# Three edits to the expert loop of a mixture-of-experts kernel: small copies on GpSimd, an early branch hint, another order of products

## The chip, the core and the metric

The kernel runs on one core of a Trainium2 chip. The metric is the time on the device in microseconds, lower is better. A core has five engines that work side by side, each with its own queue of instructions in order: TensorE (PE in the rows; PEld is its weight load), VectorE (DVE), ScalarE (ACT), GpSimd (POOL) and SyncE (SP). They wait for each other through semaphores. A letter q behind an engine's name in a row (PEldq, DVEq) is that engine's sequencer, the part that handles branches, waits and counts.

## The reference

A linear attention, a dense two-layer network and, last, a mixture of experts with 8 experts. The change touches the experts alone:

```
for b, s in tokens:
    fresh_e = argmax(logits[b, s])
    e = fresh_e if s == 0 or local_gate[b, s] < 0.5 else prev_e
    p = softmax(logits[b, s])
    h = relu(x[b, s] @ w1[e])            # 384 -> 1024
    out[b, s] = p[e] * (h @ w2[e])       # 1024 -> 384
```

There are 1536 tokens. The expert that a token goes to depends on the data, so the number of tokens of each expert is known only when the kernel runs.

## The kernel before

The first 300 us or so compute attention, the dense network and the routing; they end with a table of token ids and probabilities for each expert. One expert, which the routing prefers, has 256 of its tokens computed early, and these two results are scattered to the output from `XH` (`e2s`, line 885) at the start of the loop described here.

Then comes a loop over the experts e = 0 to 7, written out in full. Each expert's tokens are worked off in tiles of 128. Tile 0 of every expert is always done; tile t > 0 is guarded by a branch, `tc.If(nts[e] > 2 * t)`, nested in `others(e, t)`, so an expert with few tokens jumps over all of its further tiles. In this data experts 0, 1, 3 and 7 have one tile, 5 and 6 have two, 2 and 4 have three: 14 tiles in all. Where a jump is taken, each engine carries out a short join: it adds to its semaphores what the skipped tiles would have added, so that waits behind the join find the same counts on both ways.

One tile is one call of `step(e, t, before, o)`. It is software pipelined: a step does the first product of its own tile and the second product of the tile before it.

- `first_pe` multiplies the transposed rows x (128 tokens) with w1, 512 columns at a time, into banks 0 and 1. Float32 precision is made from two parts: x and w1 are split into an upper part (`xh`, `w1h`) and a lower part (`xl`, `w1l`), and each half takes nine matmuls, six with `xh` and three with `xl`.
- `first_act` (ScalarE) applies the relu and writes `hs`; in the next step `turn_pe` transposes `hs` (8 transposes into banks 2 and 3), and `turn_split` splits it: ScalarE writes the upper part into `hh`, VectorE the lower part into `hl`.
- `second` multiplies `hh` and `hl` with w2, 24 matmuls into bank 4. The result of bank 4 is fetched one step later again by `result`: ScalarE multiplies it with the tile's probability `cur_p` (line 999), and GpSimd scatters it with the ids (line 1000) to the output by an indirect DMA.
- `xpose_pe` and `xpose_split` transpose gathered rows and split them (ScalarE upper part, VectorE lower part): within the step for a further tile (t > 0), and one expert ahead for the tile 0 of the next expert. `get` issues the gather of rows, an indirect DMA on GpSimd.
- `fill2` splits the weights of the next sets into upper part (ScalarE) and lower part (VectorE, up to 1024 columns each). They are done in the steps of tile 0, six in most of them: one fill of w2 (`fl(0)`), two more of w2 (`fl(1)`), and three of w1 (`fl(2)`) near the end of the step, just ahead of `shift`.
- `shift`, at the very end of a step, moves the ids and probabilities one tile on: `cur_i`, `cur_p` take the values of `nxt_i`, `nxt_p`, and these take the ids and probabilities of the tile just done. Those are four copies of 128x1 on VectorE, and `result` copies `cur_i` into a buffer of its own (`oi`, line 998), also on VectorE.

Within the loop the order of each engine's queue is the order in which the calls are written. Ahead of `second`, a step whose `before` is not None gives TensorE a hint for the next branch: `tc.mark_branch_hint_location` places an instruction that tells TensorE early which way the branch `end{e}.{t + 1}` will go. The step (0, 0) has no `before` and thus no hint. Only TensorE gets hints.

Of the kernel before, what the change touches and what calls it, by code (L numbers as in the profile page):

```python
# [27 lines left out]
KD = DM // 128  # L28
# [3 lines left out]
JMAX = NTOK // 128  # L32
# [68 lines left out]
def moe_kernel(ctx: ExitStack, tc: tile.TileContext, rT, kT, rn, kn, vn, wt, un, gt, w_c, wg, w1, w2,  # L101
               cst, cst_b, out, dbg=None):
    nc = tc.nc
    PE, DVE, ACT, POOL, SP = nc.tensor, nc.vector, nc.scalar, nc.gpsimd, nc.sync
# [8 lines left out]
    B = [BB[:, i] for i in range(8)]  # L113
# [10 lines left out]
    tab = const.tile([128, NE, 2, JMAX + 2], F32, name="tab")  # L124
    tabj = tab[:, :, :, 0:JMAX]
    ids = const.tile([128, NE, JMAX], I32, name="ids")
# [34 lines left out]
    def load_a(e):  # L161
        if e < NE:
            for n in range(2):
                s = slice(n * 512, n * 512 + 512)
                SP.dma_start(out=raws[e % 2][0][:, :, s], in_=r3(w1[e], KD)[:, :, s])

    def load_b(e):
        if e < NE:
            for n in range(2):
                s = slice(n * 4, n * 4 + 4)  # L170
                SP.dma_start(out=raws[e % 2][1][:, s], in_=r3(w2[e], KE)[:, s])
# [20 lines left out]
    def fill2(e, i):  # L192

        a, c = raws[e % 2]
        w1h, w1l, w2h, w2l = sets[(e + 1) % 2]
        if i < 3:
            split(w1h[:, i], w1l[:, i], a[:, i])
        else:
            n = slice((i - 3) * 1024, (i - 2) * 1024)
            split(*(t.rearrange("p k f -> p (k f)")[:, n] for t in (w2h, w2l, c)))  # L200
# [5 lines left out]
    def xpose_pe(x, i):  # L206
        px = r3(B[6 + i][:, 0:DM], KD)
        for k in range(KD):
            PE.transpose(px[:, k, :], x[:, k * 128:(k + 1) * 128], ident)

    def xpose_split(i):
        s = slice(i * 128, i * 128 + 128)
        split(XQ[:, 0, :, s], XQ[:, 1, :, s], r3(B[6 + i][:, 0:DM], KD))

    if True:
# [543 lines left out]
        nts = []  # L759
# [166 lines left out]
        def rows(e, t):  # L926

            return XP[e % 2][:, t % 2] if t else XE[e % 2][:, 0]

        def get(e, t):  # L930
            if e < NE and t < JMAX:
                gather(rows(e, t), ids[:, e, t:t + 1])
# [13 lines left out]
        with tc.manual_schedule():  # L946
            for t in ORDER.split():
                name, *a = t.split(".")
                name, _, e = name.partition(":")
# [6 lines left out]
        (cur_i, nxt_i), (cur_p, nxt_p) = ((t[:, 0:1], t[:, 1:2]) for t in now)  # L956

        def shift(e, t):
            DVE.tensor_copy(out=cur_i, in_=nxt_i)  # L959
            DVE.tensor_copy(out=cur_p, in_=nxt_p)  # L960
            if e is not None:
                DVE.tensor_copy(out=nxt_i, in_=ids[:, e, t:t + 1])
                DVE.tensor_copy(out=nxt_p, in_=tab[:, e, 1, t:t + 1])

        def first_pe(e, i, n):

            w1h, w1l = sets[(e + 1) % 2][:2]
            xh, xl = XT[0]
            t, ns = slice(128 * i, 128 * i + 128), slice(n * 512, n * 512 + 512)
            todo = [(a_, w_, k) for k in range(KD) for a_, w_ in ((xh, w1h), (xh, w1l))] + [(xl, w1h, k) for k in range(KD)]  # L970
            for q, (a_, w_, k) in enumerate(todo):
                PE.matmul(out=B[n], lhsT=a_[:, k, t], rhs=w_[:, k, ns], start=(q == 0), stop=(q == 8))  # L972

        def first_act(n):
            ACT.activation(out=hs[:, n * 512:n * 512 + 512], in_=B[n], func=ACTF.Relu)

        def turn_pe(n):
            pt = r3(B[2 + n], 4)
            for k in range(4):
                f = 4 * n + k  # L980
                PE.transpose(pt[:, k, :], hs[:, f * 128:(f + 1) * 128], ident)

        def turn_split(n):
            f = slice(4 * n, 4 * n + 4)
            split(hh[:, f, 0:128], hl[:, f, 0:128], r3(B[2 + n], 4))

        def second(e):
            w2h, w2l = sets[(e + 1) % 2][2:]
            q = 0
            for n in range(2):  # L990
                for a_, w_ in ((hh, w2h), (hh, w2l), (hl, w2h)):
                    for k in range(4 * n, 4 * n + 4):
                        PE.matmul(out=B[4][:, 0:DM], lhsT=a_[:, k, 0:128], rhs=w_[:, k, :], start=(q == 0), stop=(q == 23))  # L993
                        q += 1

        def result(n):
            o, oi = XO[n]
            DVE.tensor_copy(out=oi, in_=cur_i)  # L998
            ACT.activation(out=o, in_=B[4][:, 0:DM], func=ACTF.Copy, scale=cur_p)  # L999
            POOL.indirect_dma_start(out[:, :], IndirectOffsetOnAxis(ap=oi[:, 0:1], axis=0), o[:, :], None,  # L1000
                                    bounds_check=NTOK - 1, oob_is_err=False)

        def step(e, t, before, o):

            if t:
                xpose_pe(rows(e, t), 1)
            else:
                first_pe(e, 0, 0)
            if before is not None:
                for n in range(2):  # L1010
                    turn_pe(n)
                result(o)
            if t:
                xpose_split(1)
                get(e, t + 1)
                first_pe(e, 1, 0)

            todo = [] if t or e == 0 else [(e, q) for q in range(3, 6)] + [(e + 1, q) for q in range(3) if e + 1 < NE]
            parts = todo[:1], todo[1:3], todo[3:]

            def fl(n):
                for q in parts[n]:
                    fill2(*q)

            fl(0)
            if before is not None:
                for n in range(2):
                    turn_split(n)
            first_act(0)
            first_pe(e, int(t > 0), 1)  # L1030
            fl(1)
            first_act(1)
            if t == 0 and e + 1 < NE:
                xpose_pe(rows(e + 1, 0), 0)
                xpose_split(0)
                get(e + 2, 0)
                get(e + 1, 1)
            if before is not None:

                if t + 1 < JMAX:  # L1040
                    tc.mark_branch_hint_location(f"end{e}.{t + 1}", nts[e] > 2 * t + 2, engines=[PE.engine])
                second(before)
            fl(2)
            if t == 0:
                load_a(e + 3)
                if e:
                    load_b(e + 2)
            shift(e, t)

        def others(e, t):  # L1050
            if t < JMAX:
                with tc.If(nts[e] > 2 * t, label=f"end{e}.{t}"):
                    step(e, t, e, t % 2)
                    others(e, t + 1)
# [5 lines left out]
        for e in range(NE):  # L1060
            step(e, 0, e - 1 if e else None, 2 + e % 2)
            if e + 1 < NE:
                ld_n(e + 1)
            others(e, 1)
        for n in range(2):
            turn_pe(n)
        result(2)
        for n in range(2):
            turn_split(n)
        second(NE - 1)  # L1070
        shift(None, 0)
        result(3)


# [71 lines left out]
```

## Time and profile before

| | us |
|---|---|
| median of 3 runs | 479.41 |
| lowest and highest run | 476.97, 481.84 |
| the profiled execution | 477.66 |
| its span on the core | 475.8 |

Of the span, TensorE's matmuls are busy for 83%, VectorE for 66%, ScalarE and GpSimd for 39% each. The mean granted clock of TensorE is 0.966 of full speed. Times in the rows below count from the start of the span; the expert loop is what lies behind 303 us. Of the time of the profiled execution 1.9 us lie outside its span.

### The profile page before, as it was taken

The numbers are of one execution on the slowest core, as the hardware profiler recorded it, in microseconds if no ns is written. First come the engines' busy times: TensorE is split into PE (matmuls) and PEld (weight loads), VectorE is DVE, ScalarE is ACT, GpSimd is POOL, SyncE is SP. The second block draws the span as 40 slices with busy tenths as digits, with TensorE's granted clock in tenths as the row PEclk, the third lists the DMA queues.
The fourth block names the chain that finished last, engine by engine and source line by source line (L and its number), as shares of the span: only waits on it lengthen the run. The fifth ranks groups of instructions, "written<-read, shape, count | busy, mean of one in ns | idle before, by whom it ended". The sixth has DMA issues, their size and how long they took to land. (4 is left out here: it accounts for less than half of the span.)

```text
span 475.8 us, 8791 instructions
## 1 busy us (share of the span) xinstructions
PE 395.7 (83%) x3297; PEld 359.2 (75%) x3297; DVE 315.1 (66%) x673; ACT 186.9 (39%) x447; POOL 187.6 (39%) x185
## 2 busy tenths in 40 slices
PE   1445497899989989999999889849789979989884
PEld 1444486799789979989999878737678868878774
DVE  7998999946963784787649678717912861546240
ACT  1364255221413522121325244317734752637340
POOL 6769978643622551282303220514322211212210
PEclk9999799999989999999999998959999999999997
DMA  8766165033103305000070392672861484230000
GB/s 257 276 198 210 66 221 178 1 104 120 33 2 112 113 17 171 3 34 3 9 290 3 107 391 100 209 273 65 319 242 44 129 322 152 75 106 17 9 23 15
DMA packets 24849, 59.70 MB, mean 125 GB/s; under 512 B 3994, under 2 KB 10598, under 8 KB 24512
## 3 DMA queue, kind: packets, MB, share of 16 engines
q1 hardware_dynamic: 21856, 50.85, 31.2%
q0 software_dynamic: 2912, 7.88, 4.6%
q8 instruction: 38, 0.62, 0.5%
q14 instruction: 43, 0.35, 0.2%
HBM read 56.35 MB, written 5.70 MB: 130 GB/s over the span
## 5 line engine op out<-in xcount | busy, mean ns | idle before, releaser
L515 PE MATMUL banks<-wh,H 128*128 128x384 f32 x288 | 83.9, 352 | 8.1 <-DVE H L503 6.6
L972 PE MATMUL banks<-w1h,xq 128*128 128x512 f32 x168 | 59.7, 417 | 18.3 <-ACT xq L142 9.0
L515 PEld LDWEIGHTS banks<-wh,H 128*128 128x128 f32 x288 | 53.7, 193 | 10.3 <-DVE H L503 7.5
L147 DVE TENSOR_TENSOR w2l<-wb,w2h 128x1024 fp32r<-128x1024 f32 (+1 forms) x27 | 29.3, 1108 | 45.0 <-ACT w2h L142 45.0
L972 PEld LDWEIGHTS banks<-w1h,xq 128*128 128x128 f32 x168 | 32.4, 193 | 28.5 <-ACT xq L142 9.9
L500 ACT ACTIVATE H<-banks 128x512 fp32r<-128x512 f32 x36 | 21.3, 594 | 79.2 <-PE banks L496 72.5
L515 PE MATMUL banks<-wl,H 128*128 128x384 f32 x144 | 49.3, 342 | 0.0
L993 PE MATMUL banks<-w2h,H 128*128 128x384 f32 x224 | 47.4, 345 | 0.3 <-ACT H L142 0.3
L496 PE MATMUL banks<-xq,wh 128*128 128x256 f32 x216 | 44.8, 306 | 0.4 <-DVE xq L479 0.4
L993 PEld LDWEIGHTS banks<-w2h,H 128*128 128x128 f32 x224 | 40.1, 192 | 1.2 <-ACT H L142 0.5
L496 PEld LDWEIGHTS banks<-xq,wh 128*128 128x128 f32 x216 | 36.9, 207 | 1.1 <-DVE xq L479 0.6
L1000 POOL DMA_INDIRECT out<-xh,oi x9 | 9.7, 1076 | 69.4 <-ACT xh L999 63.0
L503 DVE SCALAR_TENSOR_TENSOR H<-banks,H 128x512 fp32r<-128x512 f32 x36 | 24.5, 685 | 18.5 <-ACT H L500 18.4
L972 PE MATMUL banks<-w1l,xq 128*128 128x512 f32 x84 | 34.2, 407 | 0.3 <-DVE now_i L959 0.2
L147 DVE TENSOR_TENSOR w1l<-wa,w1h 128x512 fp32r<-128x512 f32 (+1 forms) x36 | 32.4, 951 | 0.1
L496 PE MATMUL banks<-xq,wl 128*128 128x256 f32 x108 | 32.2, 298 | 0.0
L496 PE MATMUL banks<-xuh,wh 128*128 128x256 f32 x108 | 31.3, 290 | 0.0
L496 PE MATMUL banks<-xul,wh 128*128 128x256 f32 x108 | 30.6, 284 | 0.5 <-DVE xul L479 0.5
L496 PE MATMUL banks<-xuh,wl 128*128 128x256 f32 x108 | 30.5, 282 | 0.0
L142 ACT ACTIVATE w2h<-wb 128x1024 fp32r<-128x1024 f32 (+1 forms) x33 | 28.5, 903 | 2.5 <-DMA wb<-in_w 2.5
L373 POOL TENSOR_TENSOR cv<-R,c 64x384 f32<-64x384 f32 x19 | 18.8, 992 | 23.7 <-DVE c L368 22.0
L142 ACT ACTIVATE w1h<-wa 128x512 fp32r<-128x512 f32 (+1 forms) x36 | 28.1, 856 | 0.0
(234 smaller groups left out, 948.5 us busy)
## 6 DMA issues: line engine op xcount, KB each, us to landing
wa<-in_w SPq DMA_DIRECT2D x16, 768.0 KB, 8.1
wb<-in_w SPq DMA_DIRECT2D x16, 768.0 KB, 10.6
wq<-in_w_c SPq DMA_DIRECT2D x12, 768.0 KB, 6.0
r<-in_rT SPq DMA_DIRECT2D x12, 256.0 KB, 3.3
k<-in_kT SPq DMA_DIRECT2D x12, 256.0 KB, 5.5
rn<-in_rn SPq DMA_DIRECT2D x12, 192.0 KB, 3.9
R<-in_vn SPq DMA_DIRECT2D x24, 96.0 KB, 2.5
kn<-in_kn SPq DMA_DIRECT2D x12, 192.0 KB, 3.1
```

The source lines that it names most:

```text
L142: ACT.activation(out=dst_hi, in_=src, func=ACTF.Relu if relu else ACTF.Copy)
L147: (lo_eng or DVE).tensor_tensor(out=dst_lo, in0=src, in1=dst_hi.bitcast(F32), op=ALU.subtract)
L373: e.tensor_tensor(out=r3(cv[b][s], NH), in0=r3(R[b][g % 2][s, q, :], NH), in1=bc(c[s], [64, NH, HD]), op=ALU.mult)
L496: PE.matmul(out=ph[:, i, :], lhsT=a, rhs=x_[:, k, :], start=(q == 0), stop=(q == 8))
L500: ACT.activation(out=hh[:, ring(n)], in_=r3(B[3 + n % 2], 2), func=ACTF.Relu)
L503: DVE.scalar_tensor_tensor(out=hl[:, ring(n)], in0=r3(B[3 + n % 2], 2), scalar=0.0, in1=hh[:, ring(n)].bitcast(F32), op0=ALU.max, op1=ALU. ...
L515: PE.matmul(out=bank_o(b, g), lhsT=a[:, f2, s][:, i], rhs=w_[:, 2 * p + i, DM:], start=(p + i + n == 0), stop=(p == NP - 1 and i == 1 and ...
L972: PE.matmul(out=B[n], lhsT=a_[:, k, t], rhs=w_[:, k, ns], start=(q == 0), stop=(q == 8))
L993: PE.matmul(out=B[4][:, 0:DM], lhsT=a_[:, k, 0:128], rhs=w_[:, k, :], start=(q == 0), stop=(q == 23))
L1000: POOL.indirect_dma_start(out[:, :], IndirectOffsetOnAxis(ap=oi[:, 0:1], axis=0), o[:, :], None, bounds_check=NTOK - 1, oob_is_err=False)
```

## The change

The four copies of `shift` and the copy of `result` go from VectorE's queue to GpSimd's. The hint is a function of its own, `hint(e, t)`; in the step (0, 0) it now stands ahead of the first products, and elsewhere where it stood. `first_pe` takes several halves: for a further tile (t > 0) it does the six products with `xh` of both halves, then the three with `xl` of both. For a tile 0 the order stays as it was.

```diff
         def shift(e, t):
-            DVE.tensor_copy(out=cur_i, in_=nxt_i)
-            DVE.tensor_copy(out=cur_p, in_=nxt_p)
+            POOL.tensor_copy(out=cur_i, in_=nxt_i)
+            POOL.tensor_copy(out=cur_p, in_=nxt_p)
             if e is not None:
-                DVE.tensor_copy(out=nxt_i, in_=ids[:, e, t:t + 1])
-                DVE.tensor_copy(out=nxt_p, in_=tab[:, e, 1, t:t + 1])
-
-        def first_pe(e, i, n):
+                POOL.tensor_copy(out=nxt_i, in_=ids[:, e, t:t + 1])
+                POOL.tensor_copy(out=nxt_p, in_=tab[:, e, 1, t:t + 1])
+
+        def first_pe(e, i, *halves):
...
-            todo = [(a_, w_, k) for k in range(KD) for a_, w_ in ((xh, w1h), (xh, w1l))] + [(xl, w1h, k) for k in range(KD)]
-            for q, (a_, w_, k) in enumerate(todo):
-                PE.matmul(out=B[n], lhsT=a_[:, k, t], rhs=w_[:, k, ns], start=(q == 0), stop=(q == 8))
+            t = slice(128 * i, 128 * i + 128)
+            for last in range(2):
+                todo = [(xl, w1h, k) for k in range(KD)] if last else [(xh, w_, k) for k in range(KD) for w_ in (w1h, w1l)]
+                for n in halves:
+                    for q, (a_, w_, k) in enumerate(todo):
+                        PE.matmul(out=B[n], lhsT=a_[:, k, t], rhs=w_[:, k, n * 512:n * 512 + 512],
+                                  start=(last == 0 and q == 0), stop=(last == 1 and q == KD - 1))
...
         def result(n):
             o, oi = XO[n]
-            DVE.tensor_copy(out=oi, in_=cur_i)
+            POOL.tensor_copy(out=oi, in_=cur_i)
...
+        def hint(e, t):
+
+            if t + 1 < JMAX:
+                tc.mark_branch_hint_location(f"end{e}.{t + 1}", nts[e] > 2 * t + 2, engines=[PE.engine])
+
         def step(e, t, before, o):
...
             else:
+                if before is None:
+                    hint(e, t)
                 first_pe(e, 0, 0)
...
-                first_pe(e, 1, 0)
+                first_pe(e, 1, 0, 1)
...
-            first_pe(e, int(t > 0), 1)
+            if t == 0:
+                first_pe(e, 0, 1)
...
             if before is not None:
-
-                if t + 1 < JMAX:
-                    tc.mark_branch_hint_location(f"end{e}.{t + 1}", nts[e] > 2 * t + 2, engines=[PE.engine])
+                hint(e, t)
                 second(before)
```

## Rows read from the trace of the kernel before

**Rows 1.** Waits of TensorE from 300 us on: total us, times, longest.

```profile
PE banks L972 <- ACT xq L142: 9.0, 4, 2.6
PE banks L972 <- PEq L1052: 8.0, 5, 6.3
PE banks L209 <- DMA x<-xd,ids: 3.7, 3, 1.6
```

**Rows 2.** Timeline, expert 2 into its tile 1: start, us, engine, line, operation [idle before].

```profile
337.75 2.04 ACT L142 ACTIVATE w1h<-wa 128x1024 fp32r<-128x1024 f32 x2
337.97 3.48 DVE L147 TENSOR_TENSOR w1l<-wa,w1h 128x1024 fp32r<-128x1024 f32 x3
...
339.04 1.04 PE L981 MATMUL banks<-cs,hs 128*128 128x128 f32 x8
...
341.44 0.14 DVE L960 COPY now_p<-now_p 128x1 f32<-128x1 f32 x1
...
341.66 0.58 ACT L999 ACTIVATE x<-banks,now_p 128x384 f32<-128x384 f32 x1 [1.88 <-issue]
...
342.65 0.56 DVE L147 TENSOR_TENSOR xq<-banks,xq 128x384 fp32r<-128x384 f32 x1 [0.23 <-ACT xq L142]
...
342.67 0.50 PE L972 MATMUL banks<-w1h,xq 128*128 128x512 f32 x1 [2.59 <-ACT xq L142]
...
343.23 1.03 POOL L1000 DMA_INDIRECT out<-x,oi  x1 [7.04 <-DVE xq L147]
...
344.18 0.87 PE L972 MATMUL banks<-w1h,xq 128*128 128x512 f32 x3
```

**Rows 3.** Timeline, expert 5 into its tile 1.

```profile
414.06 2.98 ACT L142 ACTIVATE w1h<-wa 128x1024 fp32r<-128x1024 f32 x3
...
416.96 1.04 PE L981 MATMUL banks<-cs,hs 128*128 128x128 f32 x8
...
418.88 0.58 ACT L999 ACTIVATE x<-banks,now_p 128x384 f32<-128x384 f32 x1 [1.84 <-PE banks L981]
...
419.89 0.50 PE L972 MATMUL banks<-w1h,xq 128*128 128x512 f32 x1 [1.90 <-ACT xq L142]
```

**Rows 4.** Timeline, the steps (1, 0) and (2, 0), after the jumps of experts 0 and 1.

```profile
319.27 0.58 ACT L999 ACTIVATE xh<-banks,now_p 128x384 f32<-128x384 f32 x1 [8.74 <-DMA out<-xh,top_i]
...
331.17 0.86 PEld L981 LDWEIGHTS banks<-cs,hs 128*128 128x128 f32 x8 [0.34 <-DVEq L1052]
...
331.20 0.58 ACT L999 ACTIVATE xh<-banks,now_p 128x384 f32<-128x384 f32 x1 [2.83 <-DVEq L1052]
```

**Rows 5.** The guard's line, 308 to 317 us: ns min/median/max, first and last start.

```profile
L1052 POOLq EVENT_SEMAPHORE  x3: 17/43/5851, 313.7 to 313.9; - x3
L1052 PEldq COMPARE_BRANCH  x1: 6236/6236/6236, 309.9 to 309.9; - x1
```

**Rows 6.** The guard's line, 455 to 463 us, the jump of expert 7.

```profile
L1052 ACTq COMPARE_BRANCH  x1: 50/50/50, 456.4 to 456.4; - x1
...
L1052 DVEq COMPARE_BRANCH  x1: 62/62/62, 459.0 to 459.0; - x1
...
L1052 DVEq EVENT_SEMAPHORE  x1: 21/21/21, 462.0 to 462.0; - x1
```

**Rows 7.** Timeline, the jump of expert 7 and behind it.

```profile
457.24 0.61 ACT L975 ACTIVATE hs<-banks 128x512 f32<-128x512 f32 x1
...
462.14 1.06 PE L981 MATMUL banks<-cs,hs 128*128 128x128 f32 x8 [1.65 <-DVEq L1052]
```

**Rows 8.** Stretch of the last products: us, busy of PE, PEld, DVE, ACT, POOL, PEclk, DMA.

```profile
464.00:468.00 4.00, 4.00 (x16) 4.00 (x15) 1.03 (x5) 0.00 (x0) 0.13 (x1) 0.57 0.02 5
```

**Rows 9.** Small GpSimd operations of line 461: ns min/median/max.

```profile
L461 POOL TENSOR_SCALAR rs<-sq x12: 190/191/596, 35.3 to 231.3; 128x1 f32<-128x1 f32 x12
```

**Rows 10.** Timeline, an operation of line 462 and VectorE beside it.

```profile
77.86 0.96 DVE L299 TENSOR_TENSOR wl<-d,wh 128x768 fp32r<-128x768 f32 x1
...
78.08 1.15 POOL L462 TENSOR_TENSOR rs<-rs,mhalf 128x1 f32<-128x1 f32 x1
```

More of the change, by code (lines that the diff above doesn't have):

```diff
@@ L958, in shift @@
         def shift(e, t):
-            DVE.tensor_copy(out=cur_i, in_=nxt_i)
-            DVE.tensor_copy(out=cur_p, in_=nxt_p)
+            POOL.tensor_copy(out=cur_i, in_=nxt_i)
+            POOL.tensor_copy(out=cur_p, in_=nxt_p)
             if e is not None:
-                DVE.tensor_copy(out=nxt_i, in_=ids[:, e, t:t + 1])
-                DVE.tensor_copy(out=nxt_p, in_=tab[:, e, 1, t:t + 1])
-        def first_pe(e, i, n):
+                POOL.tensor_copy(out=nxt_i, in_=ids[:, e, t:t + 1])
+                POOL.tensor_copy(out=nxt_p, in_=tab[:, e, 1, t:t + 1])
+        def first_pe(e, i, *halves):
             w1h, w1l = sets[(e + 1) % 2][:2]
             xh, xl = XT[0]
-            t, ns = slice(128 * i, 128 * i + 128), slice(n * 512, n * 512 + 512)
-            todo = [(a_, w_, k) for k in range(KD) for a_, w_ in ((xh, w1h), (xh, w1l))] + [(xl, w1h, k) for k in range(KD)]
-            for q, (a_, w_, k) in enumerate(todo):
-                PE.matmul(out=B[n], lhsT=a_[:, k, t], rhs=w_[:, k, ns], start=(q == 0), stop=(q == 8))
+            t = slice(128 * i, 128 * i + 128)
[5 more added lines that the diff above has]
+                                  start=(last == 0 and q == 0), stop=(last == 1 and q == KD - 1))
         def first_act(n):
```

## The prediction

> **What bounds the kernel now.** The table shows TensorE as the busiest engine, and the change touches nothing ahead of the expert loop, so I read the loop alone. First the waits of TensorE there [rows 1]. Three causes are nearly all of them: 9.0 us in four waits for ScalarE's upper part of x, 8.0 us behind the guard's branch, 6.3 of them at one place, and 3.7 us in three waits for gathered rows. All else TensorE does back to back, so a microsecond counts where it shortens one of these. Next, the timeline at each of them, to see what is late there.
>
> The four waits for x are the four entries into a tile 1 (experts 2, 4, 5 and 6). Expert 2 shows the chain [rows 2]. TensorE has finished its transposes at 339.04 + 1.04 = 340.08 and stands until 342.67. It waits for ScalarE's split of x, which is queued behind the multiplication by `cur_p` (line 999). That one starts at 341.66, just 0.08 us after `shift`'s second copy ends (341.44 + 0.14). And the copy stands in VectorE's queue behind three fills of w1l that run until 337.97 + 3.48 = 341.45. So a copy of 128 numbers holds up the product until VectorE has done its fills. ScalarE itself was free at 337.75 + 2.04 = 339.79. Expert 4 repeats the pattern of expert 2, expert 6 that of expert 5 [rows 3].
>
> **Part 1: the copies on GpSimd.** Removed from VectorE: five copies a step of about 0.15 us. Added on GpSimd: the same five, for which the nearest small operation takes 0.19 us, at worst 0.60 [rows 9]. GpSimd has its gathers and scatters and little else here; in a tile 0 its copies stand behind two gathers, in a further tile behind a scatter and a gather, each about 1 us, and the values are wanted one step (some 10 us) later. At these prices they are hidden. If that cover were gone, each microsecond that `cur_p` came after ScalarE is free would be one on the path, up to today's wait.
>
> *Entries of experts 2 and 4.* Without the wait the multiplication starts when ScalarE is free, at 339.79, and the product follows 342.67 - 341.66 = 1.01 us later as now: 340.80 for 342.67, 1.87 gained. There is more: after the jump of expert 1 ScalarE now idles 2.83 us, until 331.20, because line 999 waits for VectorE's join, which comes after its copies [rows 4]. With `cur_p` on GpSimd this goes, and ScalarE's queue, thus its fills, moves up by what TensorE's transposes allow, by my count about 0.9 us. Then TensorE's own transposes end last, and the whole 2.59 us [rows 2] go. Bounds 1.87 and 2.59; I take 2.5, since 0.9 is more than the 0.72 that are missing: 5.0 for the two.
>
> *Entries of experts 5 and 6.* Here ScalarE is free at 414.06 + 2.98 = 417.04, the product could start at 418.05, the transposes end at 416.96 + 1.04 = 418.00: 418.05 for 419.89 [rows 3]. That is 1.84, and 3.7 for two.
>
> *Third tiles (experts 2 and 4).* TensorE waits for gathered rows; of the 3.7 us [rows 1] the longest, 1.6, is in expert 0, ahead of the loop's first branch, which leaves 2.1. The gather is queued behind the scatter, and the scatter starts only at 343.23, when VectorE's split of x has ended (342.65 + 0.56), though its data were there at 342.24 [rows 2]: its wait on VectorE, for `oi`, is counted with a later instruction. With `oi` on GpSimd it goes right after line 999: about 0.7 us earlier against TensorE. But gathers share the DMA engines with the loads of weights. Bounds 0 and 2.1; I take 1.2, nearer to 0.7 for each.
>
> *Jumps of experts 1 and 3.* TensorE's transposes wait 0.34 us for VectorE's join behind the copies [rows 4]. 0.2 each, bounds 0 and 0.34: 0.4.
>
> *The last jump.* VectorE branches at 459.0, behind its copies, and joins at 462.0 [rows 6]; it has no hint. TensorE waits 1.65 us for that [rows 7]. Where nothing holds its sequencer, an engine branches ahead of its last work: ScalarE at 456.4, its last activation starts at 457.24 [rows 6, 7]. So without the copies VectorE branches once its last fill is handed over, by my estimate 1.5 us earlier, and TensorE's own last product is then as late as the join. Bounds 0.4 (the copies' own time) and 1.65; I take 1.5. Behind it, from 464 to 468, the granted clock is 0.57 [rows 8]: TensorE is at 1.2 GHz for most of it, after the 1.65 us of idling, 1.06 us of transposes and another short wait. Four microseconds at 0.57 lose 4.0 x 0.43 = 1.7. With the gap gone I expect the clock to stay up, but a gap of 1.9 to 2.6 us elsewhere lowered nothing, so I can't be sure of the link. Bounds 0 and 1.7; I take 1.5. Together 3.0.
>
> **Part 2: the hint in the step (0, 0).** The branch of expert 0 takes TensorE 6236 ns [rows 5], the largest single stall in the loop. With the hint some 6.5 us ahead of it the stall should go. I still count nearly nothing. In the next step ScalarE stands 8.74 us at line 999, until 319.27, because the buffer that it writes is being read by the scatter of the early results, whose DMA has not landed [rows 4]. Behind it in ScalarE's queue are the split of `hs`, without which `second` can't start, and all fills of this step. TensorE would do its two halves early and then wait there instead, with the clock down. What is left is ScalarE's own short wait for the transposes behind line 999, 0.4 us. Against that: line 999 now waits for GpSimd's join, and GpSimd's join there sits in a wait of 5851 ns from 313.9, until 319.75 [rows 5]. If the copies' count is added behind that wait, line 999 is 0.5 to 1.1 us late. Bounds -1.1 and +0.5; I take -0.1. Where the stall goes: to line 999, behind a scatter that the change doesn't touch.
>
> **Part 3: `xh` ahead in further tiles.** The same 18 matmuls. Today `xl` is there in time: VectorE ends it at 343.21, and TensorE, which starts at 342.67, comes to it six matmuls later, at 344.18 [rows 2]. After part 1 TensorE starts at 340.1 and VectorE's split of x still stands behind its fills: it ends between 341.1 and 342.0. The old order would come to it at 341.6, the new one six matmuls, 1.5 us, later. So this part has no price today and is what covers part 1; without it up to 0.4 us would go back at each of experts 2 and 4. The first half of `hs` comes 1.5 us later for it, and the next reader is a whole `second` away. 0.
>
> **Sum.** 5.0 + 3.7 + 1.2 + 0.4 + 3.0 - 0.1 = 13.2. The profiled execution takes 477.66; it lies 1.75 under the median of the runs. 477.66 - 13.2 = 464.5 for it, 479.41 - 13.2 = 466.2 for the median. With all lower bounds: 3.7 + 3.6 + 0 + 0 + 0.4 - 1.1 = 6.6; with all upper ones 5.2 + 3.8 + 2.1 + 0.7 + 3.35 + 0.5 = 15.7.
>
> **The rivals.**
>
> *GpSimd is locked out (474.5).* Small GpSimd operations take 0.19 us as a rule [rows 9]. One of line 462 took 1.15: it starts 0.22 us into a VectorE operation that reads two tiles in SBUF, and ends 0.41 us after it [rows 10]. The fills of w1l and w2l are such operations, back to back. If the copies get in only when VectorE pauses, `cur_p` comes when it does now, and all of the entries' 8.7 goes: 13.2 - 8.7 = 4.5, thus 474.9, or with a few collisions more 474.5 to 476. What speaks against it: in experts 5 and 6 the copies fall ahead of the fills, and one slot between two fills is enough. The Trainium skill has this as a rule (SBUF — State Buffer, section "Who interferes with whom"): a VectorE instruction with two SBUF inputs contends with a GpSimd instruction that reads SBUF, and the one that issues later blocks for the whole of the other. By that rule a waiting copy goes in at the end of a fill; the rows above agree with the blocking, and no row shows who goes first when both wait. Chance 0.12.
>
> *The hint pays in full (460).* If line 999 of the step (1, 0) did not have to wait for the scatter, the 6.3 us would go, down to 460. The wait's releaser in the trace speaks against it [rows 4]; a shift in the order of GpSimd's first DMAs would speak for it. Chance 0.07.
>
> *GpSimd's join on the path (slower, 482).* Line 999, the first work of ScalarE behind each of the 8 jumps, now needs GpSimd's join, and this queue waits at the join for its DMAs [rows 5]. Today nothing waits for it. Were it 2 us behind TensorE's join at all 8 jumps, 16 us would come on top of the gain: 479.41 - 13.2 + 16 = 482. It decides from the point where the gathers land later than TensorE ends `second`; with a wait as long as 5.85 us this is near at the jumps out of a tile 0, and far at those out of further tiles. Chance 0.06.
>
> *It doesn't do what it says (479).* The hint does not take and ScalarE waits for some other count of VectorE at the entries. The 0.08 us between copy and line 999 speak against it. Chance 0.05.
>
> **How the numbers follow.** Forecast 466.2, chance 0.70; its own range is 463 to 472.8, from the bounds of the sum. The range that I give adds the 2 us by which the runs differ and takes in most of the lock-out: 460.5 to 474.5. One per cent, 4.8 us, is about what a measurement of this kernel can tell from no change: faster is under 474.6. The forecast and the full hint are faster (0.77), and so is a part of the lock-out (0.05): 0.82. The rest of the lock-out and no effect: 0.12. Slower: the join, 0.06.
>
> **What would show it.** Right: line 999 of the entries starts as ScalarE's last fill ends, and TensorE's wait for x shrinks from 9.0 us to under 1; VectorE's last join comes before 461; the first branch is short, but line 999 of the step (1, 0) still starts near 319. Wrong: a small copy on GpSimd of a microsecond or more, line 999 released by GpSimd, or TensorE at 1.2 GHz in another place than before.

## The result and the profile after

| | before | after |
|---|---|---|
| median, us | 479.59 (4 runs) | 466.12 (4 runs) |
| lowest and highest run | 476.97, 481.84 | 465.41, 466.47 |
| the profiled execution, its span | 477.66, 475.8 | 466.47, 464.7 |
| mean granted clock | 0.966 | 0.961 |

The ratio is 0.9719, with a 95% interval of 0.9668 to 0.977: faster by 13.5 us by the medians, with a forecast of 13.2 and 466.2. In the changed kernel `shift` is at lines 959 to 963, the first products at 974, the relu at 978, the transposes of `hs` at 984, the second product at 996, `result` at 1001 (ids), 1002 (ScalarE) and 1003 (scatter), the guard at 1061.

To compare executions I count from the first product of the step (0, 0), "the loop's start" below. From there to the end of the span it is 475.8 - 303.37 = 172.43 us before and 464.7 - 305.46 = 159.24 after: 13.19 gained, to within the 0.1 us to which a span is given. A median counts every run; a ratio leaves out the few runs in a slower state of the chip (one of `early_mix`'s six).

The waits of TensorE from 300 us on in the kernel after, to be held against [rows 1] (total us, times, longest):

```profile
PE banks L974 <- ACTq L1061: 3.4, 3, 2.1
PE banks L209 <- DMA x<-xd,ids: 2.2, 2, 1.8
PE banks L974 <- PEq L1061: 1.9, 4, 0.5
PE banks L996 <- ACT H L142: 1.7, 2, 1.4
```

The wait of 9.0 us for ScalarE's part of x is gone, and of the 8.0 us behind the guard 1.9 are left. The wait for ScalarE's sequencer behind the guard has grown from 0.7 to 3.4 us, and that for ScalarE's split of `hs` ahead of the second product from 0.3 to 1.7. First the entry of expert 2 into its tile 1, in the timeline of the kernel after (start, us, engine, line, operation), against [rows 2]:

```profile
338.32 2.99 ACT L142 ACTIVATE w1h<-wa 128x1024 fp32r<-128x1024 f32 x3
...
339.09 0.17 POOL L960 COPY now_p<-now_p 128x1 f32<-128x1 f32 x1
...
339.48 3.49 DVE L147 TENSOR_TENSOR w1l<-wa,w1h 128x1024 fp32r<-128x1024 f32 x3
...
341.18 0.60 ACT L1002 ACTIVATE x<-banks,now_p 128x384 f32<-128x384 f32 x1
341.26 1.04 PE L984 MATMUL banks<-cs,hs 128*128 128x128 f32 x8
...
342.21 0.50 PE L974 MATMUL banks<-w1h,xq 128*128 128x512 f32 x1
...
342.88 0.55 DVE L147 TENSOR_TENSOR xq<-banks,xq 128x384 fp32r<-128x384 f32 x1
...
343.23 1.03 POOL L1003 DMA_INDIRECT out<-x,oi  x1 [2.49 <-ACT H L142]
...
344.57 1.03 POOL L203 DMA_INDIRECT x<-xd,ids  x1 [0.31 <-issue]
```

The probability is in place at 339.26, two microseconds before ScalarE wants it; line 1002 starts as ScalarE's last fill ends, and TensorE goes from its transposes, which end at 342.30, to the first product at 342.21 without a wait (ends are modelled). The gather for the next tile starts at 344.57, 2.36 behind that product. VectorE still has its fills in front of its split of x, and nothing of this step waits for them.

The two jumps at the loop's start look otherwise (timeline after, the steps (1, 0) and (2, 0)), against [rows 4]:

```profile
313.23 0.80 PE L974 MATMUL banks<-w1h,xq 128*128 128x512 f32 x1 [0.90 <-ACTq L1061]
...
321.07 0.58 ACT L1002 ACTIVATE xh<-banks,now_p 128x384 f32<-128x384 f32 x1 [8.21 <-DMA out<-xh,top_i]
...
323.13 0.96 PE L996 MATMUL banks<-w2h,H 128*128 128x384 f32 x4 [1.39 <-ACT H L142]
...
326.67 2.98 ACT L142 ACTIVATE w1h<-wa 128x1024 fp32r<-128x1024 f32 x3
...
327.80 3.55 DVE L147 TENSOR_TENSOR w1l<-wa,w1h 128x1024 fp32r<-128x1024 f32 x3
...
329.07 1.18 POOL L960 COPY now_p<-now_p 128x1 f32<-128x1 f32 x1
...
329.75 0.79 PE L974 MATMUL banks<-w1h,xq 128*128 128x512 f32 x1 [2.13 <-ACTq L1061]
...
331.58 0.58 ACT L1002 ACTIVATE xh<-banks,now_p 128x384 f32<-128x384 f32 x1 [1.93 <-POOLq L1061]
...
334.13 1.09 ACT L142 ACTIVATE H<-banks 128x512 fp32r<-128x512 f32 x2 [1.02 <-issue]
```

and the guard's line at the jumps of expert 0 (first row) and expert 7 (ns min/median/max, first and last start), against [rows 5, 6]:

```profile
L1061 PEldq COMPARE_BRANCH  x1: 469/469/469, 312.2 to 312.2; - x1
...
L1061 DVEq COMPARE_BRANCH  x1: 63/63/63, 448.6 to 448.6; - x1
L1061 DVEq EVENT_SEMAPHORE  x1: 21/21/21, 450.0 to 450.0; - x1
```

The hint takes: 469 ns for 6236. But line 1002 of the step (1, 0) still stands, for 8.21 us, until the early results have landed, and the second product waits behind it. At the jump of expert 1 TensorE stands 2.13 us and starts 0.10 us after ScalarE's last fill of w1h (326.67 + 2.98 = 329.65); before it was 0.10 us too (325.39 + 2.98 = 328.37, and 328.47). There the copy of the probability took 1.18 us beside VectorE's fills, and line 1002 was released by GpSimd's join. At the last jump VectorE needs 1.4 us from branch to join, 3.0 before.

Last the clock (stretches of the kernel after: us, busy of PE, PEld, DVE, ACT, POOL, PEclk, DMA), against [rows 8]:

```profile
313.00:318.00 5.00, 4.77 (x13) 3.80 (x14) 0.45 (x1) 0.00 (x0) 2.54 (x6) 0.50 1.03 394
...
329.50:334.00 4.50, 4.25 (x15) 3.44 (x16) 2.65 (x3) 1.68 (x3) 2.63 (x5) 0.62 0.36 107
...
335.00:458.00 123.00, 119.46 (x646) 105.48 (x644) 58.85 (x69) 67.07 (x105) 42.48 (x91) 1.00 0.38 138
...
454.00:458.00 4.00, 3.82 (x22) 3.50 (x21) 0.64 (x2) 0.09 (x1) 0.70 (x4) 1.00 0.02 5
```

TensorE ends at full clock now, and instead has a stretch at 0.62, thus mostly 1.2 GHz, behind its 2.13 us at the jump of expert 1. From 335 us to its end it is at full clock throughout.

### The profile page after: what moved, and what is told of

Same layout as the page of the kernel before. It is cut to its first block, busy times and chain, and to the rows that moved or that the text cites. A ratio compares the mean times of both kernels' runs of the same rounds, so it can differ in the third digit from the quotient of the medians.

```text
span 464.7 us, 8778 instructions
## 1 busy us (share of the span) xinstructions
PE 397.1 (85%) x3297; PEld 361.0 (78%) x3297; DVE 310.7 (67%) x600; ACT 186.7 (40%) x447; POOL 205.6 (44%) x258
## 5 line engine op out<-in xcount | busy, mean ns | idle before, releaser
L515 PE MATMUL banks<-wh,H 128*128 128x384 f32 x288 | 86.2, 361 | 8.7 <-DVE H L503 6.5
L974 PE MATMUL banks<-w1h,xq 128*128 128x512 f32 x168 | 61.0, 425 | 5.8 <-ACTq L1061 3.4
L515 PEld LDWEIGHTS banks<-wh,H 128*128 128x128 f32 x288 | 55.6, 199 | 11.0 <-DVE H L503 7.5
L515 PE MATMUL banks<-wl,H 128*128 128x384 f32 x144 | 50.4, 350 | 0.0
L996 PE MATMUL banks<-w2h,H 128*128 128x384 f32 x224 | 46.4, 339 | 1.7 <-ACT H L142 1.7
L496 PE MATMUL banks<-xq,wh 128*128 128x256 f32 x216 | 41.8, 292 | 0.4 <-DVE xq L479 0.4
L996 PEld LDWEIGHTS banks<-w2h,H 128*128 128x128 f32 x224 | 39.1, 188 | 2.9 <-ACT H L142 2.2
L496 PEld LDWEIGHTS banks<-xq,wh 128*128 128x128 f32 x216 | 34.4, 193 | 1.1 <-DVE xq L479 0.6
L974 PE MATMUL banks<-w1l,xq 128*128 128x512 f32 x84 | 34.8, 414 | 0.2 <-DVEq L1061 0.2
L496 PE MATMUL banks<-xq,wl 128*128 128x256 f32 x108 | 30.7, 284 | 0.0
L515 PEld LDWEIGHTS banks<-wl,H 128*128 128x128 f32 x144 | 28.8, 200 | 0.0
```

The lines of the kernel that those rows point to most:

```text
L496: PE.matmul(out=ph[:, i, :], lhsT=a, rhs=x_[:, k, :], start=(q == 0), stop=(q == 8))
L515: PE.matmul(out=bank_o(b, g), lhsT=a[:, f2, s][:, i], rhs=w_[:, 2 * p + i, DM:], start=(p + i + n == 0), stop=(p == NP - 1 and i == 1 and ...
L974: PE.matmul(out=B[n], lhsT=a_[:, k, t], rhs=w_[:, k, n * 512:n * 512 + 512], start=(last == 0 and q == 0), stop=(last == 1 and q == KD - 1))
```

## The experiments

Four questions: is it GpSimd that brings the gain, or the place in the queue; what the other two parts are worth; what the hint is lost to; and what happens to the copies beside VectorE's fills. Times are medians, ratios are to the kernel before on the same chip, and "loop" counts from the loop's start in the profiled execution (before 172.4, after 159.2).

**Each part alone.** `copies_alone` is the kernel before with the copies on GpSimd:

```diff
-            DVE.tensor_copy(out=cur_i, in_=nxt_i)
+            POOL.tensor_copy(out=cur_i, in_=nxt_i)
...
-            DVE.tensor_copy(out=oi, in_=cur_i)
+            POOL.tensor_copy(out=oi, in_=cur_i)
```

> The five small copies on GpSimd, no hint in the step (0, 0), the old order of products. Theory (the copies are the gain): ratio 0.97 to 0.975, 12 to 14 us less than before; the expert loop, from its first product to the end of the span, about 159 us against 172.4 before and 159.2 with all three edits. TensorE's waits for the upper part of x shrink from 9.0 us to under 1. Rival (the hint carries a good part): 3 us or more slower than all three edits together.

467.11 us, ratio 0.9714 (0.967 to 0.9757), loop 159.11. The whole gain is in this part. With the old order TensorE goes from the first product of expert 2's tile 1 to the second product in 4.32 us, as before and after: no wait for the lower part of x.

`hint_alone` is the kernel before with the hint in the step (0, 0):

```diff
             else:
+                if before is None:
+                    tc.mark_branch_hint_location(f"end{e}.{t + 1}", nts[e] > 2 * t + 2, engines=[PE.engine])
                 first_pe(e, 0, 0)
```

> The hint in the step (0, 0) alone. Theory (line 999 of the step (1, 0) waits for the scatter of the early results anyway): the branch goes from 6.2 us to under 0.6, the first product of the step (1, 0) starts some 5 us earlier, and the whole gains 0 to 1 us; ratio 0.998 to 1.002. Rival (the hint pays in full): 6 us less, ratio 0.987.

479.80 us, ratio 0.9988 (0.9959 to 1.0016), loop 172.9. The waits of ScalarE and of TensorE in it:

```profile
ACT xh L999 <- DMA out<-xh,top_i: 9.2, 1, 9.2
```

```profile
PE banks L993 <- ACT H L142: 2.8, 2, 2.4
```

The transposes of the step (1, 0) come 5.2 us earlier (11.72 us behind the loop's start for 16.88), the second product 1.75 (18.60 for 20.35), the first product of expert 2 not at all (25.21 for 25.10).

`no_hint` is the kernel after without this call of `hint`:

```diff
             else:
-                if before is None:
-                    hint(e, t)
                 first_pe(e, 0, 0)
```

> All three edits but the hint in the step (0, 0). Theory: as with all three, loop within 1 us of 159.2. The hint made TensorE idle twice at other places, with the clock down from 313 to 318 and again from 329.5 to 334; without it one low stretch behind the 6.2 us of the branch is left, so it may even be up to 1 us less. Rival (the hint pays once the copies are off VectorE): 3 us or more above all three edits.

466.43 us, ratio 0.971 (0.9674 to 0.9746), loop 159.04: no difference from the whole change.

`order_alone` is the kernel before with the products in the new order:

```diff
...
-                first_pe(e, 1, 0)
+                first_pe(e, 1, 0, 1)
...
-            first_pe(e, int(t > 0), 1)
+            if t == 0:
+                first_pe(e, 0, 1)
```

> The upper part of x ahead in further tiles, alone. Theory: VectorE's lower part is in time with either order, so no change: ratio 0.998 to 1.002, loop within 0.3 us of 172.4. Rival (the order saves a wait today): 0.5 us less at each of six further tiles, 3 us.

479.05 us, ratio 0.9981 (0.9951 to 1.001), loop 172.34: nothing.

**The engine or the place.** `early_shift` is the kernel before, with `shift` still on VectorE and called right behind `result`, ahead of the fills:

```diff
                 result(o)
+                shift(e, t)
...
-            shift(e, t)
+            if before is None:
+                shift(e, t)
```

> The kernel before with one edit: `shift` stays on VectorE and is called right behind `result`, ahead of the fills, not at the end of the step. Theory (what cost the time is the place in VectorE's queue, behind three fills): the four entries and the last jump gain as with the copies on GpSimd; only the gain at the third tiles, which comes from `oi`, is missing. Loop 159.5 to 161.5, ratio 0.973 to 0.978. Rival (VectorE's load or its share of the port is the cost): loop above 165.

465.02 us, ratio 0.9733 (0.9699 to 0.9767), loop 161.8, 0.3 above the range expected. At the entry of expert 2 TensorE's transposes of `hs` now start 0.94 us ahead of the first product, for 0.95 in the kernel after and 3.63 before. So for the entries the copies need not leave VectorE; they have to leave the place behind its fills. One small wait is new, in the list of TensorE's weight loads:

```profile
PEld banks L972 <- DVE xq L147: 2.1, 4, 0.5
```

Here the copy of `cur_p` waits for line 999 and VectorE's split of x stands behind it, so the old order of products comes too early for `xl`: 4.67 us from first to second product for 4.32, at four entries.

`oi_on_dve` is the kernel after with the ids for the scatter copied on VectorE:

```diff
-            POOL.tensor_copy(out=oi, in_=cur_i)
+            DVE.tensor_copy(out=oi, in_=cur_i)
```

> All three edits, but the copy of `result` (`oi`) back on VectorE. Theory (the scatter of a tile 1 waits for a later instruction of VectorE, and the gather of the third tile is queued behind it): in experts 2 and 4 the gather is issued 0.5 to 0.8 us later, TensorE's waits for gathered rows grow by 0.5 to 1.5 us, loop 159.7 to 160.7. Rival (the gather's landing is set by the loads of weights): loop within 0.3 us of 159.2.

466.97 us, ratio 0.9784 (0.9745 to 0.9823), loop 162.6, 1.9 above the range expected. At expert 2's entry (timeline):

```profile
336.44 3.48 DVE L147 TENSOR_TENSOR w1l<-wa,w1h 128x1024 fp32r<-128x1024 f32 x3
...
337.65 1.18 POOL L960 COPY now_p<-now_p 128x1 f32<-128x1 f32 x1
338.77 1.19 POOL L962 COPY now_i<-ids 128x1 int32<-128x1 int32 x1
338.86 0.58 ACT L1002 ACTIVATE x<-banks,now_p 128x384 f32<-128x384 f32 x1 [0.62 <-POOL now_p L960]
```

The lock-out of the first rival, here at an entry: the copies met three fills back to back, and each came through only once a fill had ended. ScalarE stood 0.62 us of TensorE's 2.43 there for it, and the clock fell behind that gap (5.75 us from first to second product). The gather for the third tile starts 2.61 and 2.93 us behind its tile's first product (experts 2 and 4), for 2.36 and 1.94 in the kernel after.

**What the hint is lost to.** My theory: line 1002 of the step (1, 0) writes `XH[1]`, which the scatter of the early results is still reading. The rival: it waits for GpSimd's join, where the untaken tiles' scatters are made up for. `own_buffer` gives this result another of the four buffers:

```diff
-            step(e, 0, e - 1 if e else None, 2 + e % 2)
+            step(e, 0, e - 1 if e else None, 1 if e == 1 else 2 + e % 2)
```

> All three edits, and the result of the step (1, 0) goes into another buffer, which no early scatter reads. Theory (the scatter of the early results is what makes the hint worthless): line 1002 of the step (1, 0) starts when GpSimd has joined, 13.3 us after the loop's first product and not 15.6; the loop is 1.5 to 2.5 us shorter than 159.2. Rival (the weight fills behind it set the pace anyway): loop within 0.5 us of 159.2.

465.57 us, ratio 0.9729 (0.9687 to 0.9772), loop 160.9, longer than either expectation, and the line still waits (timeline, and the guard's line):

```profile
320.13 0.58 ACT L1002 ACTIVATE x<-banks,now_p 128x384 f32<-128x384 f32 x1 [9.57 <-DMA out<-xh,top_i]
...
L1061 POOLq INC_SWDGE_SEM  x1: 408/408/408, 319.6 to 319.6; - x1
```

The timeline names the landing again, but the times do not fit it. The scatter issued at 313.24 lands 6.0 us later, at 319.2, and the line starts 0.9 us after that, 0.15 us behind the last count that GpSimd adds in its join (319.57 + 0.41 = 319.98). In the kernel after the scatter issued at 315.15 lands at 320.96, the line starts at 321.07, and that count of the join begins only at 321.51.

`early_all` is `early_shift` with the hint and this buffer, so that no copy on GpSimd is left:

```diff
+                if before is None:
+                    tc.mark_branch_hint_location(f"end{e}.{t + 1}", nts[e] > 2 * t + 2, engines=[PE.engine])
...
-            step(e, 0, e - 1 if e else None, 2 + e % 2)
+            step(e, 0, e - 1 if e else None, 1 if e == 1 else 2 + e % 2)
```

> `shift` on VectorE ahead of the fills, the hint in the step (0, 0), and the buffer of its own for the result of the step (1, 0). Theory: line 999 of the step (1, 0) then waits for VectorE's join alone, about 8.5 us after the loop's first product and not 15.6, and the 6.2 us of the branch are worth something: loop 154 to 157.5, ratio 0.962 to 0.970. Rival (TensorE's low clock or the fills take it back): loop as with the early shift alone, 160 to 161.

467.26 us, ratio 0.9783 (0.9742 to 0.9823), loop 162.2, again above both; the line waits 9.33 us, by the timeline for the same landing, by the times again until 0.15 us behind that count. By these two the buffer seemed to be out. But the buffer taken, `XR[1]`, is also written and scattered in the untaken tiles, and their count is made up for in the join: one wait was exchanged for the next. `fresh_buffer` is the kernel after with a fifth tile that nothing else uses:

```diff
-            XO.extend(zip((*XR, *XH), (cl.tile([128, 1], I32, name=f"oi{n}") for n in range(4))))
+            xo4 = cl.tile([128, DM], F32, name="xo4")
+            XO.extend(zip((*XR, *XH, xo4), (cl.tile([128, 1], I32, name=f"oi{n}") for n in range(5))))
...
-            step(e, 0, e - 1 if e else None, 2 + e % 2)
+            step(e, 0, e - 1 if e else None, 4 if e == 1 else 2 + e % 2)
```

> All of the change, but the result of expert 1's first tile goes into a buffer of its own, which no earlier scatter reads and which no skipped tile uses. What ScalarE's copy of that result waits for at its 8.2 us wait in the changed kernel is disputed. If it waits for a buffer that the scatter ahead is still reading, it now starts some 13.3 us behind the loop's first product, as GpSimd's copies are done, instead of 15.6, and the loop gets shorter by up to 2 us: 157 to 157.5 us instead of 159.2. If it waits for GpSimd's own join behind the untaken tiles, where the count of the scatters not run is made up, nothing changes: copy at 15 to 16 us, loop 159.0 to 159.5, total 465 to 467.

466.42 us, ratio 0.9722 (0.9677 to 0.9767), loop 159.3.

```profile
ACT xo L1003 <- POOLq L1062: 4.5, 1, 4.5
```

Now the line goes at GpSimd's join, 13.4 us behind the loop's start for 15.6. It was the buffer after all; the next wait in line is GpSimd's. `early_mix` has `shift` early on VectorE and all else as the kernel after:

```diff
-            POOL.tensor_copy(out=cur_i, in_=nxt_i)
+            DVE.tensor_copy(out=cur_i, in_=nxt_i)
...
                 result(o)
+                shift(e, t)
...
```

> The four copies stay on VectorE but are called right behind the result of the tile before, ahead of the fills; the copy of the ids for the scatter on GpSimd, the hint and the new order of the products as in the change. If the place in the queue was the cost and not the engine, the four entries give what the change gave (TensorE waits under 0.1 us for the lower part of x, 4.31 us from the first product of the new tile to the second product instead of the 4.65 of the early copies with the old order), and no copy can be held up by GpSimd's port: loop 158 to 159.5 us, total 464 to 466. If GpSimd is what the gain needs, the entries lose 0.3 to 2 us each again: loop over 161.

467.24 us, ratio 0.9727 (0.9669 to 0.9786), loop 158.75; 4.32 us from first to second product at the entries of experts 2 and 4, so the wait for `xl` is gone. Two edits can have done that, the new order and the copy of the ids on GpSimd: VectorE's split of x ends 1.51 us behind the first product, for 1.70 in `early_shift`, and the old order comes to it after 1.51. `early_fresh` is `early_mix` with the fifth tile:

```diff
...
-            step(e, 0, e - 1 if e else None, 2 + e % 2)
+            step(e, 0, e - 1 if e else None, 4 if e == 1 else 2 + e % 2)
```

> As the kernel with early copies on VectorE and the rest of the change, and in addition the result of expert 1's first tile has a buffer of its own. If the wait at the first jump is for the buffer and for GpSimd's copies together, ScalarE's copy of the result goes at VectorE's own join, 8.1 to 8.5 us behind the loop's first product, and the loop is 154 to 157 us, total 459 to 463. If it is for the landing of the scatter, or for GpSimd's join, by way of the copied ids or of the scatter's count, it stays at 13 to 16 us and the loop at 158 to 159.5.

464.32 us, ratio 0.968 (0.9639 to 0.9721), loop 158.7: the line moves, the loop stays. Timeline of the step (1, 0):

```profile
314.92 0.58 ACT L1003 ACTIVATE xo<-banks,now_p 128x384 f32<-128x384 f32 x1 [2.59 <-DVEq L1064]
...
322.02 0.18 POOL L1002 COPY oi<-now_i 128x1 int32<-128x1 int32 x1 [5.14 <-DMA out<-xh,top_i]
322.24 0.15 DVE L960 COPY now_i<-now_i 128x1 int32<-128x1 int32 x1 [9.00 <-POOL oi L1002]
...
324.47 1.01 PE L997 MATMUL banks<-w2h,H 128*128 128x384 f32 x2 [3.14 <-DVE H L147]
```

The line goes at VectorE's join, 9.5 us behind the loop's start. But VectorE may not overwrite `cur_i` before GpSimd has copied it, GpSimd stands behind the landing, and the lower part of `hs` stands behind VectorE. `early_split` takes this away too: `oi` on VectorE in every tile 0.

```diff
-        def result(n):
+        def result(n, V=POOL):
...
-            POOL.tensor_copy(out=oi, in_=cur_i)
+            V.tensor_copy(out=oi, in_=cur_i)
...
-                result(o)
+                result(o, POOL if t else DVE)
```

> As the kernel with early copies on VectorE and a buffer of its own for expert 1's first result, and the copy of the ids for the scatter is on VectorE as well in every expert's first tile, and on GpSimd in the further ones. In that kernel VectorE stood 9.0 us behind GpSimd's copy of the ids, which waited for a scatter to land, and gave back there the 3.4 us by which the second product had started earlier. If that copy is what is late next, VectorE now goes on at its own join, some 9.5 us behind the loop's first product, the second product of expert 0's third tile runs through without a wait, the first product of expert 2 starts 19.5 to 22 us behind the loop's first product instead of 24.7, and the loop is 153.5 to 156.5 us: total 459 to 463. If the landing of the scatter comes out again at the next jump (GpSimd's gathers for expert 2's further tiles, or a buffer that is still being scattered), the start of expert 2's second tile stays at 35 to 36 us and the loop at 158 to 159.5, total 464 to 466.

466.96 us, ratio 0.9759 (0.9716 to 0.9802), loop 159.4.

```profile
335.30 1.03 POOL L1004 DMA_INDIRECT out<-xh,oi  x1 [6.21 <-ACT w1h L142]
...
341.85 1.04 POOL L1004 DMA_INDIRECT out<-x,oi  x1 [1.76 <-DMA out<-xh,oi]
343.19 1.02 POOL L203 DMA_INDIRECT x<-xd,ids  x1 [0.30 <-issue]
...
349.54 0.55 PE L209 MATMUL banks<-cs,x 128*128 128x128 f32 x3 [2.64 <-DMA x<-xd,ids]
```

Where the time went is seen in the positions (us behind the loop's start, from the timelines):

| | line of `result` (1, 0) | second product (1, 0) | first product (2, 0) | first product (2, 1) | transposes of `hs` (2, 2) |
|---|---|---|---|---|---|
| before | 15.9 | 20.4 | 25.1 | 39.3 | 49.7 |
| after | 15.6 | 17.7 | 24.3 | 36.8 | 45.9 |
| `fresh_buffer` | 13.4 | 17.0 | 22.1 | 34.8 | 45.1 |
| `early_fresh` | 9.5 | 14.3 | 24.7 | 35.8 | 44.6 |
| `early_split` | 10.1 | 16.8 | 21.4 | 32.8 | 44.6 |

`early_split` is 4.0 us ahead of the kernel after at expert 2's tile 1, and 1.3 ahead one tile later. GpSimd's queue moved along by only 1.2 us: the scatter of 341.85 goes when the one of 335.30 has landed (341.02), the gather for expert 2's third tile stands behind it, and TensorE waits 2.64 us for its rows. Behind that gap the clock falls (5.74 us from first to second product for 4.32), and the last 1.3 us are gone. The loop stays 2.9 us above the range expected. The hint's 6 us are lost to a chain of waits: the buffer, GpSimd's join, GpSimd's copy of the ids, the scatters themselves, and at last the clock. No version here beats the change by more than the runs differ; `early_fresh`, the lowest, has an interval that overlaps.

## Why the prediction was right, and which of its steps were not

The terms below are differences of positions in the two loops: how much more the kernel after is ahead at the end of a stretch than at its start.

**Entries of experts 2 and 4:** 5.0 forecast, 5.46 measured, 2.73 each. **Entries of experts 5 and 6:** 3.7 and 3.92. The mechanism holds: at expert 2's entry line 1002 starts as ScalarE's last fill ends, and the wait for x is gone from TensorE's list. `early_shift` shows that the place behind three fills was the cause, and not that VectorE runs the copy.

**Third tiles:** 1.2 forecast, 1.65 measured, and the step was wrong. I had the gather go 0.7 us earlier against TensorE with `oi` on GpSimd. It goes 2.36 and 1.94 us behind its tile's first product; before it went at 1.89 and 1.97. The scatter ahead of it does start earlier where nothing else holds it (0.38 us behind the product at expert 4, for 0.65), but the gather does not follow; at expert 2 the scatter has to wait for the landing of the one before, at 342.40. What differed is the landing: from that product to the third tile's transposes it is 10.36 and 9.76 us in the profile of before, but 9.17 and 9.33 in `order_alone` and 9.51 and 9.42 in `hint_alone`, with the gather at the same place, 9.13 and 9.35 after, and 10.26 and 10.41 in `fresh_buffer`. So this term lies within what differs between executions. What `oi` on GpSimd does is another thing: with the entry early and `oi` left on VectorE the gather would come up to 1.0 us later (`oi_on_dve`).

**The last jump:** 1.5 forecast, 1.34 measured. VectorE needs 1.4 us from branch to join for 3.0, and TensorE waits 0.3 for 1.65.

**The clock behind it:** 1.5 forecast, 1.58 in the two profiles. The gain is real, its place was luck. In `hint_alone` the same gap of 1.6 us stands at the last jump and the clock does not fall there; it fell behind the entries of experts 5 and 6 (stretches of its third entry and of its last products):

```profile
421.00:425.00 4.00, 4.00 (x12) 3.08 (x12) 2.00 (x8) 1.16 (x3) 2.04 (x2) 0.57 0.12 37
...
466.00:471.00 5.00, 4.66 (x29) 4.45 (x30) 1.69 (x6) 1.63 (x3) 1.00 (x1) 1.00 0.02 5
```

At both it cost 1.54 us (5.85 from first to second product for 4.31), and so it did in `order_alone`. From expert 2's tile 1 on, each of the three kernels with the old waits has such a low stretch behind one of them, or behind two; the nine kernels that have lost these waits are at full clock to TensorE's end, and the two that got a new one have a low stretch behind it (`oi_on_dve` 2.43 us, `early_split` 2.64). So the clock goes with these waits, for 1.6 to 3.1 us in all, but no row tells behind which of them it falls. The mean over the whole span, 0.966 before and 0.961 after, hides this: it takes in the stretches ahead of the loop and the two low ones at the loop's start.

**The hint and the jumps of experts 1 and 3:** +0.3 forecast (0.4 and -0.1), -0.08 measured. That the hint pays nothing was right, and so was the reason, the buffer under the scatter; `hint_alone` and `no_hint` show the one, `fresh_buffer` and `early_fresh` the other, on a second try, since `own_buffer` had spoken against it. But this one wait was not all that stood in the way. The second product of the step (1, 0) is 2.67 us further ahead than before, the first product of (2, 0) only 0.80: it waits for ScalarE's fills of w1h, which stand behind line 1002, as the forecast had said. What the forecast missed is the clock behind that wait: the first nine matmuls, at 1.2 GHz for most of it, take 3.69 us for 2.70, and the 0.80 is gone. At the jump of expert 3 0.10 is gained.

**Part 3:** worth nothing, as said. Its reason was wrong: it doesn't cover part 1. In the kernel after VectorE's split of x ends at 343.43, 1.2 us behind the first product, and six matmuls take 1.5, so the old order does as well (`copies_alone`). With the copies early on VectorE and `oi` there too the old order costs 0.35 us at each entry (`early_shift`); whether the new order alone would cover that was not run, since `early_mix` moves `oi` as well.

**The lock-out**, the rival at 0.12, exists: it held ScalarE at one place of the kernel after (1.93 us, the jump of expert 1) and at one of `oi_on_dve` (0.62, expert 2's entry). At that place of the kernel after it cost TensorE nothing: ScalarE's next split stood another 1.02 us, since the transposes that it reads begin only at 333.44, and from these to the second product it is 3.24 us, for 3.29 before. That is also what became of the rival at 0.06, GpSimd's join on the path: line 1002 was released by it there, and in `fresh_buffer` for 2.59 us, with the same 3.24 behind it. The copies of the probability in the kernel after (ns min/median/max, first and last start):

```profile
L960 POOL COPY now_p<-now_p x15: 174/177/1178, 317.6 to 454.4; 128x1 f32<-128x1 f32 x15
```

A copy alone takes 0.18 us; one that meets a fill takes up to 1.18, as long as the fill, and the next fill does not hold it a second time. The Trainium skill (SBUF — State Buffer, section "Who interferes with whom") says that the one issued later blocks for the whole of the other; these rows agree. Its price in the forecast, all of the entries' 8.7, would have needed copies that never get in between two fills. All three signs that the prediction had named for being wrong stand at the jump of expert 1: a copy of over a microsecond, line 1002 released by GpSimd, and 1.2 GHz in a new place. Of these only the third cost time there.

**The tail**, unforeseen: TensorE ends 13.80 us earlier and the span 13.19. From the last product's end to the end of the span it is about 6.3 us in every kernel with the last `oi` on VectorE and 6.8 to 6.9 in every one with it on GpSimd. The last scatter starts 0.77 us after its data, 0.28 before:

```profile
457.91 0.58 ACT L1002 ACTIVATE xh<-banks,now_p 128x384 f32<-128x384 f32 x1 [4.09 <-issue]
459.26 0.98 POOL L1003 DMA_INDIRECT out<-xh,oi  x1 [4.56 <-ACT xh L1002]
```

The copy itself had long been done; what the scatter waits for in that half microsecond is open. With 0.09 lost ahead of the step (7, 0) the terms make 5.46 + 3.92 + 1.65 + 1.34 + 1.58 - 0.08 - 0.09 - 0.61 = 13.17 of the 13.19. That the sum met the forecast to 0.1 us is in part luck: the entries gave 0.7 and the third tiles 0.45 more than forecast, the jumps and the tail 1.2 less, and the 1.65 of the third tiles lies within what differs between executions. A slip without consequence: the upper bounds, 15.7, put the lower end of the sum's range at 463.7 and not at 463.

## What to carry to other kernels

A tiny operation that another engine waits for costs what stands ahead of it in its queue: look where it is issued before you look which engine runs it, since calling `shift` earlier on the same engine brought the same gain at the entries as another engine. Before a stall is removed, follow what its successor waits for, and then the next one: here four waits stood one behind the other up to a queue of scatters, and each removal moved the loss on by one. A releaser that a profile names is to be held against the times: the line that seemed to wait for a landing started 0.9 us after it, right behind a join. Of a term that a single pair of profiles seems to confirm, ask a kernel that doesn't touch it, here those with one part alone: the landing of the gather moved as much where nothing of it was changed, and the low clock stood at another gap.

## What the runs showed that was not expected

- The stretch ahead of the loop, the same code in all kernels, ended between 301.8 and 309.1 us in the profiled executions. `copies_alone`, `no_hint` and the kernel after have spans of 468.2, 464.8 and 464.7 us and loops of 159.11, 159.04 and 159.24: what differs between them lies ahead of the loop.
- Giving a result another buffer is not enough if the untaken tiles of a guard use that buffer too: the wait came back, now behind GpSimd's join, and only a tile that no guarded code touches was free.
- A hint to one engine takes its branch from 6236 to 469 ns. By the Trainium skill (Runtime: NRT & Kernel Launch, section "Instruction fetch mechanics") a taken branch to a page that isn't loaded has to fetch it first. The DMA view agrees: of the queue q8, whose kind it gives as instruction, it has one packet within the branch before (309.9 to 316.2 us, first row), which starts at 313.6; in the kernel after it has one ahead of the branch (308 to 312.2, second row), which starts at 308.5, and none within it. In all five kernels without the hint such a packet starts 3.5 to 3.8 us into this branch, in all nine with it 3.2 to 3.7 us ahead. For which engine the packet is, the view does not say.

```profile
q8 instruction: 1, 0.02, 1.1%
...
q8 instruction: 1, 0.02, 2.3%
```
